# Attention with a gated dense layer on one core: another exponential polynomial on VectorE, sums in smaller parts, and 37 groups in place of 35

## The chip, the core and the metric

The kernel runs on one core of a Trainium2 chip. A core has five instruction streams: TensorE (PE, matrix products), VectorE (DVE), ScalarE (ACT), GpSimd (POOL) and SyncE (SP, which starts DMAs). Each runs its instructions in order, and they meet only at semaphores. The metric is the device time of one execution in microseconds (us). The kernel before takes 459.85 us, the median of 3 runs (459.81 to 459.92).

## The reference

For a sequence of S = 2048 rows of width D = 448, with H = 16 heads of 28 columns and a hidden width F = 1792:

```python
xn = layernorm(x)
q, k, v = split(xn @ wqkv)                       # 16 heads of 28
p = softmax(q @ k.T * 28 ** -0.5)                # per head, 2048 x 2048
s = (p @ v) @ wo
h = gelu(xn @ w1 + b1)                           # 2048 x 1792
g = silu(h @ w2 + b2)
out = x + s * g
```

## The kernel before, in words

**Tiles.** The 16 heads are four groups of four (g), the 2048 queries four chunks of 512 (c). One pair (g, c) is a block, 16 in all, block b = 4 g + c. In a block there are 16 key tiles t of 128 keys by 4 heads j, so 64 score tiles of 128 keys by 512 queries, numbered m; over all blocks 1024. The last block is cut into pieces of 256 and 128 queries, so that its sums end sooner. Four successive tiles, the four heads of one key tile, are a quad: quad q holds tiles 4q to 4q+3.

**Two ways to the exponential.** Scores are made on TensorE, four heads beside each other as row tiles, into PSUM (L1237, `t_score`). ScalarE takes the tiles of most quads in units of two or three (`p_exps`, L1293): one ACTIVATE with Exp from the PSUM ring to a bf16 slot in SBUF (P, or space of h and xnT that is free at the time). The quads listed in `QUADS` go to VectorE instead and are called late groups: 35 of 256. `p_late` gets a free PSUM bank for each of their tiles, `p_apass` (L1396) turns a tile into a bf16 bit pattern, by adding in the exponent's place, so that it reads as 2^i (1 + f), where i is the whole and f the fractional part of the scaled score. Four such tiles lie side by side in one buffer T of 128x2048. Then `p_expq` makes two more buffers of that size:

```python
W  = T & 0x407F                    # L1447: 2 (1 + f)
D1 = W * A3/4 + A2/2               # L1449
W  = W * D1                        # L1451: a polynomial in f
D1 = T & 0x7F80                    # L1452: 2^i
W  = W * T                         # L1454
```

The exponential is T + D1 + W. The three are not added on VectorE: TensorE sums all three with the same values v.

**Sums.** `p_pv` walks the tiles in steps of 8 (two quads), behind the exponentials. `pv_task` (matmuls at L1508) makes one task of TensorE from the 8 tiles and from the late groups of that block that are ready: 4 matmuls for a quad that ScalarE made, 12 for a late group. Heads lie side by side as column tiles of the accumulator `acc`, the weights are 32 columns of `vaug` (v of a head, and a column of 2.0 that gives the softmax's denominator). At a block's end `p_epi` copies `acc` out (L1566), takes the reciprocal (L1576), splits it on GpSimd into a high and a low bf16 part (rhi L1578, rlo L1579), and TensorE spreads it (L1588).

**Other work.** Projections of q, k, v (L748, L1039), the first dense layer (`p_f1`, L1101), the gelu in one stretch in the middle (`p_gelu`, L1150; it begins at the unit that reaches tile `GM` = 582), the second dense layer (`p_f2`, L1171; its result gets b2 added on VectorE, L1177), the output projection (L1605). All of these share two PSUM banks with the late groups' tiles; six banks are the ring with units of three and two tiles, one is `acc`. `p_busy` fills spare time of TensorE with matmuls that add zero to `acc` (L909), where the planner's count of its recent use is low.

**Order.** The program is written out when the kernel is built. `_Kernel.run` is a planner: it holds a set of processes, each of which offers its next task with an estimated duration, estimates the earliest start from when its operands are ready and its engine is free, and puts down the earliest (within `EPS` = 0.1 the one with the lowest priority number). The order on each engine is then fixed, and `deps` adds the semaphore waits. A changed duration or an added task thus moves the order of work on every engine. DMAs are issued at the point of the program where their process reaches them, most on SP.

**Buffers.** Late groups need three of the twelve units of `self.unit` (space of x, plx, w2, wq, wk and, once a head group is done, kT). They are free again when the group's sum is put down.

Of the kernel before, what the change touches and what calls it, by code (L numbers as in the profile page):

```python
# [8 lines left out]
ALU = mybir.AluOpType  # L9
# [10 lines left out]
C = 4  # L20
# [7 lines left out]
MTOT = NBLK * T * 4  # L28

GM = 64 * 9 + 6  # L30
QUADS = (17, 18, 25, 37, 41, 58, 68, 70, 81, 90, 97, 98, 117, 124, 131, 135, 140, 142, 146, 154, 157, 159, 161, 162, 165, 183, 185, 197, 200, 210, 211, 225, 229, 234, 242)
SM_SCALE = DH ** -0.5
LOG2E = 1.4426950408889634
EXP_A3, EXP_A2, EXP_LC = 0.16391228, 0.00783292, 1.1187538523466403
EXP_OFF = 64.0 / (LOG2E * SM_SCALE)
LN_EPS = 1e-5
KNORM = 2.5
# [11 lines left out]
JOINT = 0.05  # L49
LEAD, WAIT, GLEAD = 0, 3.0, 48  # L50
EPS = 0.1


class _Buf:
# [22 lines left out]
class _Kernel:  # L77
# [21 lines left out]
    def sb(self, name, shape, dtype=dt.bfloat16):  # L99
        return self.es.enter_context(self.nc.sbuf_tensor(name, shape, dtype))  # L100
# [163 lines left out]
    def alloc(self):  # L264
# [30 lines left out]
        self.colK = sb("colK", [128, G], f32)  # L295
        self.plx = sb("plx", [128, 2048], bf)
        self.coff = sb("coff", [128, 1], f32)
        self.b2b = sb("b2b", [128, D], bf)
        self.st6 = sb("st6", [128, T, 6], f32)
        self.mv = sb("mv", [128, T, 2], f32)  # L300
        self.lnv = sb("lnv", [128, T], f32)
# [49 lines left out]
        self.b_qT = [[B() for _ in range(C)] for _ in range(G)]  # L351
        self.b_onT = self.b_qT
        self.q_ready = [[False] * C for _ in range(G)]
        self.b_v = [[B() for _ in range(T)] for _ in range(2)]
        self.b_h = [B() for _ in range(C)]
        self.b_g = [B() for _ in range(C)]
# [33 lines left out]
    def schedule(self):  # L390
        K = self
        K.n_f1 = 0
        K.exp_u = -1
        K.exp_m = -1
        K.late_ready = []
        K.sc_u = -1
        K.pv_m = -1
        K.E_done = -1
        K.norms_done = False
        K.stg_done = 0  # L400
        K.pe_wait = 0
# [12 lines left out]
        K.next_m = 0  # L414
        K.n_late = 0
        K.gu = None
        K.pend = None
        K.units = []
        K.pv_done = [False] * MTOT
        K.late = {4 * q + k for q in QUADS for k in range(4)}  # L420
        K.late_left = [sum(1 for q in QUADS if K.sub_of(4 * q) == b) for b in range(NBLK + 3)]
        K.late_on = False
        K.PB, K.PPREV, K.plast = {}, {}, {}
        K.free_u = []
        K.a_left = {}
        K.ln2e = 0
        K.late_blk = 0
        K.banks += [(K.ring[:, b, :], K.b_ring[b]) for b in (3, 2)]
        K.outs = []
        K.gelu_done = False  # L430
        K.dir_n = 0
        K.dir_read = 0
        self.constants()
        self.loads()
        for c in range(C):
            K.spawn(K.p_ln(c), c)
        K.spawn(K.p_first(), 0)
# [24 lines left out]
        for c in range(C):  # L462
            K.spawn(K.p_k(1, c), nxt())
        K.spawn(K.p_q(1, 0), nxt())
        for t in range(T):
            K.spawn(K.p_v1(t), nxt())
        for c in (1, 2, 3):
            K.spawn(K.p_q(1, c), nxt())
        K.spawn(K.p_qn(1), nxt())
        f1 = deque(SBT)  # L470
        for c in range(C):
            for _ in range(4):
                K.spawn(K.p_f1(*f1.popleft()), nxt())
            K.spawn(K.p_k(2, c), nxt())
            K.spawn(K.p_q(2, c), nxt())
        K.spawn(K.p_qn(2), nxt())
        while f1:
            K.spawn(K.p_f1(*f1.popleft()), nxt())
        for c in range(C):
            K.spawn(K.p_k(3, c), nxt())  # L480
            K.spawn(K.p_q(3, c), nxt())
        K.spawn(K.p_qn(3), nxt())
        K.spawn(K.p_gelu(), 0)
        K.spawn(K.p_direct(), 0)
        for c in range(C):
# [104 lines left out]
    def loads(self):  # L590
# [20 lines left out]
            ld(K.x_sb[:, c, :, :], xr[c], K.s_x[c], [K.b_x[c]], 8.0 + 1.8 * c)  # L611
        lw(4 * DH, D, K.s_wqk1, K.b_stg1, 16.5)

        ld(K.b2b[:, :], K.B_b2.partition_broadcast(128), K.s_w["b"], [K.b_b2], 20)
        ld(K.w1[:, 0:3, :], K.B_w1[0:384, :].rearrange("(kt p) f -> p kt f", p=128), K.s_w["w1"], [], 0)
        ld(K.w1[0:64, 3, :], K.B_w1[384:448, :], K.s_w["w1"], [K.b_w1], 30)

# [7 lines left out]
        def late_w2():  # L625
# [4 lines left out]
                    K.b_w2.r += b.r + [b.w]  # L630
            ld(K.w2[:, :, :], K.B_w2.rearrange("(ft p) d -> p ft d", p=128), K.s_w["w2"], [K.b_w2], K.now + 14)
        K.spawn(late_w2(), 50)

        def pool_pads():
            yield ("until", lambda: K.stg_done == 2)
# [525 lines left out]
    def p_f2(self, c, t):  # L1161
# [5 lines left out]
        for q in range(7):  # L1167
            def f(eng, q=q):
                ins = None
                for ft in (2 * q, 2 * q + 1):  # L1170
# [3 lines left out]
            yield _Task(PE, f, [K.b_w2, K.b_h[c]], [tok], 0.378, 0.17)  # L1174
        K.pe_wait -= 1
        fb = K.fsb[:, c % 2, t, :]
        yield _Task(DVE, lambda eng: eng.tensor_tensor(fb, ps, K.b2b[:, :], ALU.add), [tok, K.b_b2], [K.b_fsb[c % 2]],  # L1177
                    0.63, 0.0, 2)
        K.banks.append((bank, tok))
        K.f2n[c] += 1  # L1180
# [251 lines left out]
    def p_expq(self, m0, u):  # L1432
        K = self
        b = K.sub_of(m0)
        uv = []
        yield ("until", lambda: K.ln2e == 0 and K.a_left[m0] == 0 and K.unit_of(b) is not None)
        K.ln2e = 1
        for _ in range(2):
            yield ("until", lambda: K.unit_of(b) is not None)
            v = K.unit_of(b)  # L1440
            K.free_u.remove(v)
            uv.append(v)
# [6 lines left out]
        yield _Task(DVE, lambda eng: eng.tensor_scalar(D1.bitcast(f16), W, EXP_A3 / 4.0, EXP_A2 / 2.0, op0=ALU.mult, op1=ALU.add),  # L1449
                    bW, bD, 0.69, 0.0, 4)  # L1450
        yield _Task(DVE, lambda eng: eng.tensor_tensor(W.bitcast(f16), W, D1.bitcast(f16), ALU.mult), bW + bD, bW, 1.22, 0.0, 4)  # L1451
        yield _Task(DVE, lambda eng: eng.tensor_scalar(D1.bitcast(u16), T.bitcast(u16), 0x7F80, None, op0=ALU.bitwise_and),  # L1452
                    bT + bW, bD, 0.69, 0.0, 4)
        yield _Task(DVE, lambda eng: eng.tensor_tensor(W, W.bitcast(f16), T, ALU.mult), bT + bW, bW, 1.22, 0.0, 4)  # L1454
        K.ln2e = 0
        K.late_ready.append((m0, (u, uv[0], uv[1])))

    def p_pv(self):
        K = self
# [27 lines left out]
    def pv_task(self, q, late, ms):  # L1487
# [2 lines left out]
        for x in late:  # L1490
            K.late_ready.remove(x)
        K.late_left[b] -= len(late)
        src = [(m,) + K.p_slot(m) for m in ms if m not in K.late]
        for m0, us in late:
            for u in us:
                src += [(m0 + k, K.unit[u][:, 512 * k:512 * k + 512], K.b_U[u][k]) for k in range(4)]
        n = len(src) / 4
        fl, rd = [], []
        for kk in range(4):
            for m, ap, tok in src:  # L1500
# [6 lines left out]
                def f(eng, t=t, j=j, g=g, q0=q0, nq=nq, col=col, ap=ap):  # L1507
                    return eng.matmul(K.acc[32 * j:32 * j + 32, q0:q0 + nq], K.vaug[:, t, 4 * g + j, :],  # L1508
                                      ap[:, col:col + nq], tile_position=(0, 32 * j), start=(t == 0),
                                      stop=(t == T - 1), skip_group_check=True)  # L1510
                fl.append(f)
                rd += [tok, K.b_v[0 if g == 0 else 1][t]]

        if not src:
            return
# [6 lines left out]
        yield _Task(PE, fall, rd, [K.b_acc], 0.223 * n + 0.001 * len(fl), 0.17,  # L1522
                    lambda: 1.2 if K.exp_m - K.pv_m > 20 or K.exp_m > MTOT - 12 or (K.gu is not None and K.gu - 1 <= K.exp_u <= K.gu) else 6, mode="col")
        for _, us in late:
            K.free_u += us

    def p_slot(self, m):
        i = self.PB[m]
# [170 lines left out]
```

## Time and profile before

| | |
|---|---|
| median of 3 runs | 459.85 us |
| profiled execution | 459.7 us |
| its span, first to last instruction | 457.9 us |
| ScalarE busy | 445.3 us, 97% |
| TensorE busy | 432.7 us, 94%, of which L909 35.1 |
| VectorE busy | 381.3 us, 83% |
| GpSimd busy | 45.0 us, 10% |
| first exponential starts, last ends | 12.59, 451.27 us |
| gelu with its two table loads | 247.96 to 275.85 us |
| TensorE's granted clock | 0.997 |

Times in the profile are counted from the first instruction. Busy time is the union of an engine's instructions; durations of neighbours on one engine overlap a little, so distances from start to start say more on throughput than mean durations. TensorE's ends are modelled. In rows of groups the fields are line, engine, operation, result and operands by name, their shapes, the count, then busy us and mean ns of one, then idle time of the engine just before them and what ended it. In a list of waits the fields after the colon are total us, count and the longest.

### The profile page before, as it was taken

The page shows a single profiled execution, that of the slowest core. Times are in us where ns is not written, and L with a number is a line of the kernel's source. Part 1 is how long each engine was busy: PE and PEld are TensorE (multiplying, and loading weights), DVE is VectorE, ACT ScalarE, POOL GpSimd, SP SyncE. Part 2 cuts the span into 40 slices and gives each one's busy share as a digit, 9 for nine tenths or more (in the row PEclk, how much of TensorE's full clock was granted, in tenths as well). Part 3 has the DMA queues.
Part 4 walks back from the last instruction along what each step waited for, and adds up shares of the span by engine and source line. Part 5 has one row for each costly group of instructions (what it writes and reads, how often), then busy time and mean ns, then how long its engine had stood idle before and what let it go on. Part 6 is the DMA issues. An engine that isn't in the chain of part 4 may idle for free.

```text
span 457.9 us, 10674 instructions
## 1 busy us (share of the span) xinstructions
PE 432.7 (94%) x4446; PEld 164.0 (36%) x4475; DVE 381.3 (83%) x593; ACT 445.3 (97%) x406; POOL 45.0 (10%) x85
## 2 busy tenths in 40 slices
PE   6999999999999999999999999999999999999995
PEld 4533334332223233223234333333233333343562
DVE  8956988886878888968899898889878798889865
ACT  6999999999999999999999999999999999999994
POOL 7470000000000100100000001010000100111012
PEclk9999999999999999999999999999999999999998
DMA  8701000000000000000040000000000000402012
GB/s 265 273 2 35 4 0 1 1 1 4 1 0 1 1 3 2 3 1 1 0 140 5 2 0 1 2 1 1 0 1 2 1 1 1 82 1 34 10 23 62
DMA packets 8049, 11.16 MB, mean 24 GB/s; under 512 B 1697, under 2 KB 6993, under 8 KB 7954
## 3 DMA queue, kind: packets, MB, share of 16 engines
q1 hardware_dynamic: 6850, 8.43, 5.8%
q0 software_dynamic: 864, 1.38, 2.4%
q8 instruction: 35, 0.57, 0.5%
q10 hardware_dynamic: 288, 0.69, 0.4%
q14 instruction: 12, 0.10, 0.1%
HBM read 8.61 MB, written 3.21 MB: 26 GB/s over the span
## 4 chain that ended last, share of the span: by engine, by line
PE 53%; ACT 31%; issue 11%; DVE 3%; DMA 1%; POOL 0%; ACTq 0%; DVEq 0%; POOLq 0%
PE ring L1237 16%; ACT P L1293 14%; PE acc L1508 9%; ACT h L1293 7%; ACT xnT L1293 7%; PE ring L1101 6%; PE ring L1171 4%; PE acc L909 4%; PE ring L748 3%; PE misc L1101 2%; PE misc L748 2%; PE misc L1039 1%; ACT h L1150 1%; PE misc L1171 1%; PE ring L1039 1%
## 5 line engine op out<-in xcount | busy, mean ns | idle before, releaser
L1293 ACT ACTIVATE P<-ring 128x1024 bf16<-128x1024 f32 (+1 forms) x186 | 214.8, 1267 | 1.4 <-PE ring L1237 1.3
L1237 PE MATMUL ring<-qT,kT 32*128 32x512 bf16 (+2 forms) x1075 | 145.4, 358 | 11.3 <-ACT P L1293 4.1
L1293 ACT ACTIVATE h<-ring 128x1024 bf16<-128x1024 f32 (+1 forms) x103 | 118.4, 1242 | 0.4 <-PE ring L1237 0.2
L1237 PEld LDWEIGHTS ring<-qT,kT 32*128 32x128 bf16 x1075 | 37.5, 91 | 133.0 <-ACT P L1293 52.6
L1293 ACT ACTIVATE xnT<-ring 128x1536 bf16<-128x1536 f32 (+1 forms) x71 | 82.4, 1282 | 0.1
L1508 PE MATMUL acc<-P,vaug 128*32 128x512 bf16 (+2 forms) x526 | 48.4, 356 | 0.0
L1101 PE MATMUL ring<-xnT,w 128*128 128x512 bf16 x152 | 40.6, 382 | 1.8 <-issue 1.1
L1578 POOL CAST rhi<-rc 128x16 bf16<-128x16 f32 x15 | 5.9, 394 | 357.6 <-DVE rc L1576 333.6
L1171 PE MATMUL ring<-w,h 128*128 128x448 bf16 x154 | 37.4, 355 | 0.0
L909 PE MATMUL acc<-ident,zero 128*128 128x128 bf16 x429 | 35.1, 220 | 0.0
L909 PEld LDWEIGHTS acc<-ident,zero 128*128 128x128 bf16 x429 | 24.3, 98 | 15.4 <-issue 14.5
L1237 PE MATMUL misc<-qT,kT 32*128 32x512 bf16 (+1 forms) x77 | 28.7, 377 | 0.0
L1508 PE MATMUL acc<-h,vaug 128*32 128x512 bf16 x250 | 28.0, 384 | 0.0
L1396 DVE TENSOR_SCALAR x_sb<-ring 128x512 uint16<-128x512 f32 x26 | 17.9, 687 | 2.8 <-PE ring L1237 2.6
L1101 PEld LDWEIGHTS ring<-xnT,w 128*128 128x128 bf16 x164 | 12.3, 97 | 20.1 <-issue 7.7
L1508 PE MATMUL acc<-xnT,vaug 128*32 128x512 bf16 (+2 forms) x232 | 18.1, 333 | 0.0
L1508 PEld LDWEIGHTS acc<-P,vaug 128*32 128x32 bf16 x526 | 12.0, 94 | 16.0 <-issue 13.4
L1566 DVE CAST E_sb<-acc 128x512 bf16<-128x512 f32 x15 | 10.4, 692 | 8.3 <-PE acc L1508 8.3
L1171 PEld LDWEIGHTS ring<-w,h 128*128 128x128 bf16 x154 | 11.2, 97 | 17.1 <-issue 10.3
L1396 DVE TENSOR_SCALAR kT<-misc 128x512 uint16<-128x512 f32 x20 | 13.8, 688 | 4.1 <-PE misc L1237 4.1
L1396 DVE TENSOR_SCALAR x_sb<-misc 128x512 uint16<-128x512 f32 x22 | 15.1, 686 | 2.4 <-PE misc L1237 2.1
L1101 PE MATMUL misc<-xnT,w 128*128 128x512 bf16 x54 | 15.9, 382 | 0.9 <-issue 0.6
(281 smaller groups left out, 682.1 us busy)
## 6 DMA issues: line engine op xcount, KB each, us to landing
w<-in_B_w_dram SPq DMA_DIRECT2D x1, 1568.0 KB, 7.4
w<-in_B_w_dram SPq DMA_DIRECT2D x1, 1344.0 KB, 8.2
out_dram<-in_A_x_dram SPq DMA_DIRECT2D x3, 448.0 KB, 11.2
out_dram<-h POOLq DMA_DIRECT2D x6, 224.0 KB, 3.9
x_sb<-in_A_x_dram SPq DMA_DIRECT2D x2, 448.0 KB, 5.8
h<-in_A_wqkv_dram SPq DMA_DIRECT2D x3, 168.0 KB, 4.9
x_sb<-in_A_x_dram ACTq DMA_DIRECT2D x1, 448.0 KB, 4.4
h<-in_A_x_dram SPq DMA_DIRECT2D x1, 448.0 KB, 3.4
```

Source lines behind the costliest of these rows:

```text
L748: ins = eng.matmul(bank, w[:, kt, g * 128:(g + 1) * 128], K.xnT[:, kt, c * 512:(c + 1) * 512], start=(kt == 0), stop=(kt == KT - 1))
L909: ins = eng.matmul(K.acc[:, 0:128], K.zero[:, :], K.ident[:, :], start=False, stop=True, skip_group_check=True)
L1039: ins = eng.matmul(bank[:, off:off + nh * 32], K.xnT[:, kt, t * 128:(t + 1) * 128], ap, start=(kt == 0), stop=(kt == KT - 1), skip_group_c ...
L1101: ins = eng.matmul(bank, K.w1[:, kt, ft * 128:(ft + 1) * 128], K.xnT[:, kt, c * 512:(c + 1) * 512], start=(kt == 0), stop=(kt == KT - 1))
L1150: yield _Task(ACT, lambda eng, dst=dst, src=src: eng.activation(dst, src, ACTF.Gelu_apprx_tanh), rd, wr, 0.4267 * n + (0.1 if pc else 0.06 ...
L1171: ins = eng.matmul(ps, hv[:, ft, t * 128:(t + 1) * 128], K.w2[:, ft, :], start=(ft == 0), stop=(ft == FT - 1))
L1237: return eng.matmul(dst, K.kT[32 * j:32 * j + 32, g, t * 128:(t + 1) * 128], K.qT[32 * j:32 * j + 32, g, c * 512 + q0:c * 512 + q0 + nq], ...
L1293: return eng.activation(reg[:, i0:i0 + n, :], K.ring[:, b0:b0 + n, :], ACTF.Exp, scale=SM_SCALE)
L1396: yield _Task(DVE, lambda eng: eng.tensor_scalar(K.unit[u][:, 512 * k:512 * k + 512].bitcast(dt.uint16), bank, SM_SCALE * LOG2E * 128.0, ( ...
L1508: return eng.matmul(K.acc[32 * j:32 * j + 32, q0:q0 + nq], K.vaug[:, t, 4 * g + j, :], ap[:, col:col + nq], tile_position=(0, 32 * j), sta ...
L1566: yield _Task(DVE, lambda eng: eng.tensor_copy(E, K.acc[:, :]), [K.b_acc], [tE], 0.7, 0.0, 0)
L1578: yield _Task(POOL, lambda eng: eng.tensor_copy(K.rhi[:, :], K.rc[:, :]), [K.b_rc], [K.b_rhl], 1.1, 0.0, 1)
```

## The change

The polynomial becomes 2^i (1 + m + c m^3) with m = 1 + f (not the tile number) and c = 0.167. `p_expq` then needs two masks and two products, and no multiply-add: D1 = W W, W = D1 T, D1 = T & 0x7F80. The factor c/4 of the third operand isn't applied to W but to the values: `p_cv`, a new process on GpSimd, writes c/4 times the four heads' values of the group's key tile into one of four slots `cv` (two slots for a group of the last block), and the sum of W uses those as its weights. A late group begins its polynomial only once such slots are free and its values are there; the slots come free with the units.

The sum task is cut: `pv_task` still collects the same tiles, but gives them to `t_pv` in parts of at most `4 * PVN` = 8 tiles (two operand groups of four), each a task of its own, between which the planner may put others.

`QUADS` is a new list of 37 groups. `b2b` (b2 spread over the partitions) loses its own buffer and lies in that of `wv`; its load moves from the start to after the last use of `wv`.

```diff
-QUADS = (17, 18, 25, 37, 41, 58, 68, 70, 81, 90, 97, 98, 117, 124, 131, 135, 140, 142, 146, 154, 157, 159, 161, 162, 165, 183, 185, 197, 200, 210, 211, 225, 229, 234, 242)
+QUADS = (17, 21, 24, 33, 39, 49, 52, 66, 75, 85, 86, 98, 100, 114, 124, 134, 138, 142, 146, 153, 154, 155, 161, 162, 171, 178, 179, 189, 194, 197, 206, 210, 211, 225, 227, 237, 243)
-EXP_A3, EXP_A2, EXP_LC = 0.16391228, 0.00783292, 1.1187538523466403
+EXP_C, EXP_LC = 0.1669921875, 1.1155446
+NCV = 4
+PVN = 2
...
-        self.b2b = sb("b2b", [128, D], bf)
+        self.b2b = self.wv[:, 0, 0:D]
+        self.cv = sb("cv", [128, NCV, 128], bf)
...
-        ld(K.b2b[:, :], K.B_b2.partition_broadcast(128), K.s_w["b"], [K.b_b2], 20)
...
+        def late_b2():
+            yield ("until", lambda: all(x.tw is not None for x in K.b_v[1]))
+            K.b_b2.r += K.b_wv.r + K.b_wvpad.r + [K.b_wv.w, K.b_wvpad.w]
+            ld(K.b2b, K.B_b2.partition_broadcast(128), K.s_w["b"], [K.b_b2], K.now + 6)
+        K.spawn(late_b2(), 50)
...
-        yield ("until", lambda: K.ln2e == 0 and K.a_left[m0] == 0 and K.unit_of(b) is not None)
+        room = lambda: [i for i in range(0, NCV, len(pc)) if all(k in K.free_cv for k in range(i, i + len(pc)))]
+        yield ("until", lambda: K.ln2e == 0 and K.a_left[m0] == 0 and K.unit_of(b) is not None and room()
+               and all(bv[p[0]].tw is not None for p in pc))
...
+        K.spawn(K.p_cv(cs, [p[0] for p in pc], g, bv), m0)
...
-        yield _Task(DVE, lambda eng: eng.tensor_scalar(D1.bitcast(f16), W, EXP_A3 / 4.0, EXP_A2 / 2.0, op0=ALU.mult, op1=ALU.add),
-                    bW, bD, 0.69, 0.0, 4)
-        yield _Task(DVE, lambda eng: eng.tensor_tensor(W.bitcast(f16), W, D1.bitcast(f16), ALU.mult), bW + bD, bW, 1.22, 0.0, 4)
+        yield _Task(DVE, lambda eng: eng.tensor_tensor(D1.bitcast(f16), W, W, ALU.mult), bW, bD, 1.22, 0.0, 4)
+        yield _Task(DVE, lambda eng: eng.tensor_tensor(W, D1.bitcast(f16), T, ALU.mult), bT + bD, bW, 1.22, 0.0, 4)
...
-        yield _Task(DVE, lambda eng: eng.tensor_tensor(W, W.bitcast(f16), T, ALU.mult), bT + bW, bW, 1.22, 0.0, 4)
...
+    def p_cv(self, cs, ts, g, bv):
+        K = self
+        for i, t in zip(cs, ts):
+            yield _Task(POOL, lambda eng, i=i, t=t: eng.tensor_scalar(
+                K.cv[:, i, :], K.vaug[:, t, 4 * g:4 * g + 4, :].rearrange("p h e -> p (h e)"), EXP_C / 4.0, None, op0=ALU.mult),
+                [bv[t]], [K.b_cv[i]], 0.8)
...
+        for i in range(0, len(src), 4 * PVN):
+            yield self.t_pv(q, src[i:i + 4 * PVN])
+        for _, us, cs in late:
+            K.free_u += us
+            K.free_cv += cs
...
+                w = K.vaug[:, t, 4 * g + j, :] if cs is None else K.cv[:, cs[kk], 32 * j:32 * j + 32]
```

More of the change, by code (lines that the diff above doesn't have):

```diff
@@ L353, in alloc @@
         self.q_ready = [[False] * C for _ in range(G)]
+        self.b_cv = [B() for _ in range(NCV)]
         self.b_v = [[B() for _ in range(T)] for _ in range(2)]
@@ L424, in schedule @@
         K.free_u = []
+        K.free_cv = list(range(NCV))
         K.a_left = {}
@@ L1176, in p_f2 @@
         fb = K.fsb[:, c % 2, t, :]
-        yield _Task(DVE, lambda eng: eng.tensor_tensor(fb, ps, K.b2b[:, :], ALU.add), [tok, K.b_b2], [K.b_fsb[c % 2]],
+        yield _Task(DVE, lambda eng: eng.tensor_tensor(fb, ps, K.b2b, ALU.add), [tok, K.b_b2], [K.b_fsb[c % 2]],
                     0.63, 0.0, 2)
@@ L1435, in p_expq @@
         uv = []
-        yield ("until", lambda: K.ln2e == 0 and K.a_left[m0] == 0 and K.unit_of(b) is not None)
-        K.ln2e = 1
+        _, _, pc, _, _ = K.pieces(m0)
+        bv = K.b_v[0 if m0 // 64 < C else 1]
+        room = lambda: [i for i in range(0, NCV, len(pc)) if all(k in K.free_cv for k in range(i, i + len(pc)))]
+        yield ("until", lambda: K.ln2e == 0 and K.a_left[m0] == 0 and K.unit_of(b) is not None and room()
+               and all(bv[p[0]].tw is not None for p in pc))
+        K.ln2e = 1
+        cs = list(range(room()[0], room()[0] + len(pc)))
+        for i in cs:
+            K.free_cv.remove(i)
+        g = m0 // 64 // C
+        K.spawn(K.p_cv(cs, [p[0] for p in pc], g, bv), m0)
         for _ in range(2):
@@ L1448, in p_expq @@
                     bT, bW, 0.69, 0.0, 4)
-        yield _Task(DVE, lambda eng: eng.tensor_scalar(D1.bitcast(f16), W, EXP_A3 / 4.0, EXP_A2 / 2.0, op0=ALU.mult, op1=ALU.add),
-                    bW, bD, 0.69, 0.0, 4)
-        yield _Task(DVE, lambda eng: eng.tensor_tensor(W.bitcast(f16), W, D1.bitcast(f16), ALU.mult), bW + bD, bW, 1.22, 0.0, 4)
+        yield _Task(DVE, lambda eng: eng.tensor_tensor(D1.bitcast(f16), W, W, ALU.mult), bW, bD, 1.22, 0.0, 4)
+        yield _Task(DVE, lambda eng: eng.tensor_tensor(W, D1.bitcast(f16), T, ALU.mult), bT + bD, bW, 1.22, 0.0, 4)
         yield _Task(DVE, lambda eng: eng.tensor_scalar(D1.bitcast(u16), T.bitcast(u16), 0x7F80, None, op0=ALU.bitwise_and),
                     bT + bW, bD, 0.69, 0.0, 4)
-        yield _Task(DVE, lambda eng: eng.tensor_tensor(W, W.bitcast(f16), T, ALU.mult), bT + bW, bW, 1.22, 0.0, 4)
         K.ln2e = 0
-        K.late_ready.append((m0, (u, uv[0], uv[1])))
+        K.late_ready.append((m0, (u, uv[0], uv[1]), cs))
+    def p_cv(self, cs, ts, g, bv):
[4 more added lines that the diff above has]
+                [bv[t]], [K.b_cv[i]], 0.8)
     def p_pv(self):
@@ L1492, in pv_task, with t_pv @@
         K.late_left[b] -= len(late)
-        src = [(m,) + K.p_slot(m) for m in ms if m not in K.late]
-        for m0, us in late:
+        src = [(m,) + K.p_slot(m) + (None,) for m in ms if m not in K.late]
+        for m0, us, cs in late:
             for u in us:
-                src += [(m0 + k, K.unit[u][:, 512 * k:512 * k + 512], K.b_U[u][k]) for k in range(4)]
+                src += [(m0 + k, K.unit[u][:, 512 * k:512 * k + 512], K.b_U[u][k], cs if u == us[2] else None) for k in range(4)]
+        for i in range(0, len(src), 4 * PVN):
[3 more added lines that the diff above has]
+            K.free_cv += cs
+    def t_pv(self, q, src):
+        K = self
         n = len(src) / 4
@@ L1499, in pv_task @@
         for kk in range(4):
-            for m, ap, tok in src:
+            for m, ap, tok, cs in src:
                 _, j, pc, _, s = K.pieces(m)
@@ L1505, in pv_task, with f @@
                 t, q0, nq, col = pc[kk]
-                def f(eng, t=t, j=j, g=g, q0=q0, nq=nq, col=col, ap=ap):
-                    return eng.matmul(K.acc[32 * j:32 * j + 32, q0:q0 + nq], K.vaug[:, t, 4 * g + j, :],
+                w = K.vaug[:, t, 4 * g + j, :] if cs is None else K.cv[:, cs[kk], 32 * j:32 * j + 32]
+                def f(eng, t=t, j=j, w=w, q0=q0, nq=nq, col=col, ap=ap):
+                    return eng.matmul(K.acc[32 * j:32 * j + 32, q0:q0 + nq], w,
                                       ap[:, col:col + nq], tile_position=(0, 32 * j), start=(t == 0),
@@ L1511, in pv_task @@
                 fl.append(f)
-                rd += [tok, K.b_v[0 if g == 0 else 1][t]]
-        if not src:
-            return
+                rd += [tok, K.b_v[0 if g == 0 else 1][t] if cs is None else K.b_cv[cs[kk]]]
         def fall(eng, fl=fl):
@@ L1521, in fall @@
             return ins
-        yield _Task(PE, fall, rd, [K.b_acc], 0.223 * n + 0.001 * len(fl), 0.17,
+        return _Task(PE, fall, rd, [K.b_acc], 0.223 * n + 0.001 * len(fl), 0.17,
                     lambda: 1.2 if K.exp_m - K.pv_m > 20 or K.exp_m > MTOT - 12 or (K.gu is not None and K.gu - 1 <= K.exp_u <= K.gu) else 6, mode="col")
-        for _, us in late:
-            K.free_u += us
     def p_slot(self, m):
```

## The prediction

> **What bounds the kernel now.** I read the page's busy shares first, then the table of stretches, ScalarE's waits, the groups by shape, and the timelines around ScalarE's gaps. The table of stretches gives, for each stretch in us, its length and the busy time of TensorE (PE), its weight loads (PEld), VectorE (DVE), ScalarE (ACT) and GpSimd (POOL):
>
> ```profile
> 0.00:15.00 15.00, 10.43 (x92) 7.61 (x93) 12.62 (x46) 10.06 (x25) 10.62 (x31) 1.00 0.85 269
> ...
> 180.00:245.00 65.00, 61.42 (x615) 20.63 (x622) 54.76 (x83) 65.00 (x58) 2.57 (x6) 1.00 0.09 26
> 245.00:276.00 31.00, 30.33 (x192) 10.99 (x191) 28.80 (x40) 30.94 (x23) 0.00 (x0) 1.00 0.00 1
> 276.00:340.00 64.00, 62.87 (x596) 21.55 (x592) 54.30 (x73) 63.97 (x56) 2.91 (x6) 1.00 0.01 1
> ...
> 445.00:458.00 13.00, 7.70 (x167) 4.29 (x163) 7.47 (x16) 6.74 (x7) 3.05 (x3) 0.89 0.28 59
> ```
>
> ScalarE is full from 15 to 445 us (idle sum of those stretches about 1.5 us). VectorE has some 10 us of idle in each 64 us and GpSimd is nearly empty. So the end is set by the first exponential (12.59 us), ScalarE's stream of work, and the chain after the last exponential at 451.27 us (6.6 us: sum, reciprocal, projection, store). ScalarE's own waits say the same; the one wait inside the stream, for scores, is 1.5 us in all:
>
> ```profile
> ACT P L678 <- DMA x_sb<-in_A_x_dram: 2.2, 1, 2.2
> ACT P L1293 <- PE ring L1237: 1.3, 4, 0.5
> ...
> ACT h L1293 <- PE ring L1237: 0.2, 1, 0.2
> ```
>
> The exponentials by shape (count, then busy us and mean ns), of two and three score tiles of 128x512 each:
>
> ```profile
> L1293 ACT ACTIVATE P<-ring 128x1536 bf16<-128x1536 f32 x85 | 127.4, 1499 | 0.4 <-PE ring L1237 0.3
> L1293 ACT ACTIVATE P<-ring 128x1024 bf16<-128x1024 f32 x101 | 105.5, 1071 | 1.1 <-PE ring L1237 1.0
> ```
>
> With the rows that write h and xnT there are 85+44+35 = 164 of three and 101+59+36 = 196 of two: 884 of the 1024 tiles, the other 140 being VectorE's 35 groups. Neighbours overlap, so the price is start to start: an undisturbed exponential of two takes 0.904 us and of three 1.330 us (medians over the start times in ScalarE's timeline). 196 and 164 of these make 395.3 us; the pitches recorded sum to about 8 us more. About 1.3 us of that is small work between them at the start, the rest hiccups too short to show as idle.
>
> **What the skill says.** "SBUF — State Buffer", section "SBUF: two separate sides": VectorE and GpSimd share a port pair as an exclusive lock, held for a whole instruction, and the loser blocks. The trace agrees: GpSimd's small step rlo takes 0.22 us alone, and 1.21 us where it meets the 1.23 us product.
>
> ```profile
> 183.34 1.23 DVE L1451 TENSOR_TENSOR x_sb<-x_sb,w 128x2048 f16<-128x2048 bf16 x1
> ...
> 183.43 1.21 POOL L1579 TENSOR_TENSOR rlo<-rc,rhi 128x16 bf16<-128x16 f32 x1
> ```
>
> "TensorEngine Tiling (Array Packing)", "Key Properties": a change of tiling mode drains TensorE. In the trace a sum starts 0.31 us after a score's start, 0.1 us more than 512 columns need (0.213 us apart in a row of sums). "VectorE: DVE Perf Modes", "Side-by-side: where the cycles go for N=2048 bf16": 1224 ns for a two-input operation, 693 ns for a one-input one; the rows below agree.
>
> **The change, part by part.**
>
> *Two more groups.* 8 score tiles leave ScalarE: two exponentials of three and one of two, 2 x 1.330 + 0.904 = 3.56 us. All other ScalarE work stays. In both lists 18 groups lie before the gelu (tile 582), so all of this saving falls after 275.85 us, where 17 groups become 19.
>
> *VectorE's polynomial.*
>
> ```profile
> L1396 DVE TENSOR_SCALAR x_sb<-ring 128x512 uint16<-128x512 f32 x26 | 17.9, 687 | 2.8 <-PE ring L1237 2.6
> L1449 DVE TENSOR_SCALAR x_sb<-kT 128x2048 f16<-128x2048 bf16 x6 | 4.1, 681 | 0.1
> L1451 DVE TENSOR_TENSOR kT<-kT,x_sb 128x2048 f16<-128x2048 bf16 x6 | 7.3, 1217 | 0.0
> ```
>
> A group costs 4 x 0.687 for its score tiles, three one-input passes of 0.69 and two products of 1.22: 7.26 us. The pass of L1449 goes, the products stay two, 16-bit in and out as before: 6.57 us. In all 35 x 7.26 = 254.1 becomes 37 x 6.57 = 243.1, 11 us less. It is worth nothing by itself, since VectorE isn't the bound; it makes room for the two groups. After the gelu the balance is 17 x 7.26 = 123.4 against 19 x 6.57 = 124.8: 1.4 us more, beside about 27 us of idle there.
>
> *Scaled values on GpSimd.* 37 groups, 38 passes of 128x128 (one group lies in the last block and has two). The trace lacks this shape: a 128x128 copy (selb) took 0.29 us, a 128x128 comparison (ident) 0.62. I take 0.35; with the lock a pass may be held by each VectorE operation that it meets. Low end 0.3 us, hidden; high end the whole sequence, 3.8 us. Even then it is ready no later than the group's last operand (D1), since both start together; the sum waits for that anyway. Ahead of rhi and rlo in GpSimd's queue it can delay an epilogue, and TensorE behind its broadcast L1588, by up to about 1.5 us: a chance in some one or two of 15 blocks. The other side of the lock: 38 x 0.35 = 13 us of VectorE held at worst, against 77 us of idle; so hidden too. No recorded VectorE duration is longer beside GpSimd work.
>
> *TensorE.* Each group adds 8 sum tiles beyond those that its P tiles would need: 2 x 8 x 0.213 / 4 columns side by side = 0.85 us, and its scores, part of them taken along with ScalarE's, up to 2 x 4 x 0.22 = 1.8 us less 0.7 for three exponentials' scores. Cover: the filling matmuls (L909), 429 of 0.055 us = 24 us, of which about 12 us after the gelu.
>
> *Sums in parts.* In TensorE's order of work there are 45 unbroken runs of sums over 8 matmuls (16 of 12, 10 of 16, 18 of 20, one of 40), so about 64 new cuts. Where nothing slips in, a cut is free; where a score does, it costs two drains, 0.2 us: 0 to 13 us of TensorE, under that cover. The gain: a run of 20 takes 1.07 us and can hold a score back. At 78.5 us it does, and ScalarE loses 0.38 us:
>
> ```profile
> 78.52 0.62 PE L1508 MATMUL acc<-P,vaug 128*32 128x512 bf16 x8
> ...
> 79.72 0.62 PE L1237 MATMUL ring<-qT,kT 32*128 32x512 bf16 x6
> ...
> 80.17 1.45 ACT L1293 ACTIVATE P<-ring 128x1536 bf16<-128x1536 f32 x1 [0.27 <-PE ring L1237]
> ```
>
> Of ScalarE's hiccups over 0.07 us, ten come with a run of 12 or more, 2.2 us together, one of 0.37 at the gelu's table load perhaps not for that reason. So the parts are worth between 0 and -2 us; the new order of everything can bring hiccups of about 1 us. I take -0.6 net.
>
> *b2's load.* It goes from SP's early queue (0.61 us of issue at 8.45) to behind the last use of wv near 96 us. SP then waits there; behind it is only the next write to qT, issued at 108.7. W1's load, next in the early queue, starts 0.6 us sooner. VectorE reads b2 after 276 us. Nothing on the path: 0, either way below 0.2.
>
> *Sum*: profiled execution 459.7 (span 457.9) - 3.56 - 0.6 = 455.5; the median of the runs shown is 0.15 above the profiled time, so 455.6 us.
>
> **Rivals.** (1) *Half the gain is eaten*: two groups more after the gelu, where TensorE shows 62.87 of 64.00 us busy, give late scores. Loss of 1.5 to 3 us of new hiccups: 457 to 458.9. For it: the dense TensorE; against it: filling matmuls still fit there (27 up to 340 us), and projections can slide to 400-445, where 144 of them stand. (2) *No change* (458.9 to 460.8): TensorE's drains use up the cover, and what ScalarE loses equals the 3.56 us; I see no stretch dense enough for that. (3) *Slower*: GpSimd's passes arrive late, because the lock lets them in only after the polynomial and they then take over 1 us, and TensorE stands at a sum for them with the scores queued behind it. Only two units of scores are buffered, so a stop hurts ScalarE from about 0.5 us on. 37 stops lose over 3.56 us once each holds ScalarE by over 0.1 us, a stop of 0.6 us. With 1 us each: 37 x 0.5 - 3.6 = 15 us slower, 470. Against it: GpSimd got in between VectorE operations in every case seen, so the pass should end some 2 us ahead of its sum. (4) *More gain*: nearly all hiccups of long runs vanish too, 453.7.
>
> **How the numbers follow.** Forecast with its own range 454.2 to 457: 0.62. Rival 1: 0.18. No change: 0.05. Slower: 0.09. More gain: 0.06. Under 0.2% (0.9 us) two medians of this kernel can't be told apart; so faster 0.86, same 0.05, slower 0.09. The range 453.8 to 458.6 holds the forecast, most of rival 1 and nearly all of rival 4, leaving out about 0.18.
>
> **What would show it.** Right: ScalarE's exponentials are 162 of three and about 195 of two, its time from the first exponential after the gelu to the last falls from 175.4 to about 172 us, the gelu begins within 1 us of 247.96, VectorE's busy time falls to about 370, L1508's runs are at most 8 long between scores, and the tail after the last exponential stays 6.6 us. Wrong: idle of ScalarE or of sums waiting for the scaled values by more than 1 us in all; passes on GpSimd over 3 us; VectorE's products off 1.22 us; or hiccups after the gelu growing by more than 2 us.

## The result, and the profile after

The changed kernel takes 458.55 us (median of 4 runs, 458.24 to 459.04) against 459.88 us of the kernel before on the same chip: ratio 0.997, interval 0.9953 to 0.9988. It is faster, by 1.3 us, where 4.3 us had been forecast. Run once more on another occasion it took 458.28 us against 459.97, ratio 0.9964 (0.9952 to 0.9977).

The profiled executions are 459.7 us before (span 457.9) and 458.85 us after (span 457.0), so the spans differ by 0.9 us. ScalarE is the engine that is full from the first exponential to the last, so its own landmarks cut the span into five pieces: up to the first exponential, on to the table load of the gelu, the gelu up to the first exponential behind it, on to the end of the last exponential, and the tail.

| us | first exp | before the gelu | gelu | after the gelu | tail | span |
|---|---|---|---|---|---|---|
| before | 12.59 | 235.36 | 27.89 | 175.43 | 6.63 | 457.90 |
| after | 12.87 | 234.60 | 30.19 | 171.78 | 7.54 | 456.97 |
| difference | +0.28 | -0.76 | +2.30 | -3.65 | +0.91 | -0.93 |

The expected saving is there (-3.65), and two thirds of it are given back in the gelu stretch. The first column is not the change's: over the runs below it lies between 12.56 and 13.16, and the two executions of the changed kernel have 12.87 and 12.75.

The stretches of the changed kernel, columns as before:

```profile
245.00:276.00 31.00, 30.03 (x213) 11.11 (x215) 28.03 (x38) 28.97 (x21) 4.59 (x7) 1.00 0.00 1
276.00:340.00 64.00, 63.12 (x541) 20.95 (x539) 46.78 (x63) 63.84 (x57) 6.79 (x10) 1.00 0.01 1
```

From 245 to 276 us ScalarE was busy for 30.94 us before and is for 28.97 now. Its waits name the place; the first line is new:

```profile
ACT h L1160 <- PE ring L1111: 2.0, 2, 1.1
ACT P L1303 <- PE ring L1247: 1.0, 3, 0.5
```

L1160 is the gelu, L1111 the first dense layer. The gelu reads 34 of its 56 tiles from h in SBUF, where they were put earlier, and 22 "direct" ones straight from the ring; in that stretch TensorE must make those 22 while ScalarE works through the rest. The end of the gelu, ScalarE's timeline (start, length, instruction, idle before it and what ended it), before:

```profile
270.75 1.52 ACT L1150 ACTIVATE h<-h 128x1536 bf16<-128x1536 bf16 x1
272.13 2.40 ACT L1150 ACTIVATE h<-ring 128x1536 bf16<-128x1536 f32 x2
```

and after:

```profile
270.39 1.48 ACT L1160 ACTIVATE h<-h 128x1536 bf16<-128x1536 bf16 x1
272.74 1.45 ACT L1160 ACTIVATE h<-ring 128x1536 bf16<-128x1536 f32 x1 [0.88 <-PE ring L1111]
275.32 1.02 ACT L1160 ACTIVATE h<-ring 128x1024 bf16<-128x1024 f32 x1 [1.12 <-PE ring L1111]
```

The last two direct units come late. Before, TensorE made their 20 matmuls in one run (second line: L1101 from 268.87 to 273.36), with 16 sum matmuls behind them:

```profile
268.56 0.39 PE L1237 MATMUL misc<-qT,kT 32*128 32x512 bf16 x1
268.87 4.49 PE L1101 MATMUL ring<-xnT,w 128*128 128x512 bf16 x20
273.30 0.40 PE L1508 MATMUL acc<-P,vaug 128*32 128x512 bf16 x4
```

After, the same matmuls are parted by the epilogue of block 8 (L1617, eight pieces, of which one is shown) and by 12 sum matmuls:

```profile
268.76 2.33 PE L1111 MATMUL ring<-xnT,w 128*128 128x512 bf16 x10
271.03 0.24 PE L1617 MATMUL ring<-ident,rhi 128*32 128x128 bf16 x4
...
271.81 1.67 PE L1111 MATMUL ring<-xnT,w 128*128 128x512 bf16 x7 [0.16 <-issue]
273.42 0.40 PE L1542 MATMUL acc<-wk,vaug 128*32 128x512 bf16 x4
273.65 0.39 PE L1542 MATMUL acc<-x_sb,vaug 128*32 128x512 bf16 x4
273.86 0.39 PE L1542 MATMUL acc<-plx,cv 128*32 128x512 bf16 x4
274.18 1.04 PE L1111 MATMUL ring<-xnT,w 128*128 128x512 bf16 x4
```

In TensorE's order, between the first and the last direct matmul, there stood 36 sum matmuls and no epilogue before; now 60 and 36 epilogue matmuls. An estimate from the trace: the 24 more sum matmuls take 24 x 0.053 = 1.3 us (four columns share 0.213), the epilogue 0.5, and five more changes of tiling mode (30 against 25 between those two matmuls) at the prediction's 0.1 us another 0.5. Together these are the 2.3 us. Block 8, with three late groups (quads 134, 138, 142) in place of four (131, 135, 140, 142), now ends inside the gelu; before, it ended behind it (the step rhi of that block ran at 282.38, now at 268.43). That the list is the reason isn't shown: in e2 below, with the four groups of before, rhi ran at 272.85, inside the gelu too.

### The profile page after: what moved, and what is told of

Same layout as the page of the kernel before. It is cut to its first block, busy times and chain, and to the rows that moved or that the text cites. A ratio compares the mean times of both kernels' runs of the same rounds, so it can differ in the third digit from the quotient of the medians.

```text
span 457.0 us, 10602 instructions
## 1 busy us (share of the span) xinstructions
PE 432.2 (95%) x4397; PEld 160.6 (35%) x4428; DVE 369.8 (81%) x574; ACT 441.1 (97%) x403; POOL 70.0 (15%) x123
## 4 chain that ended last, share of the span: by engine, by line
PE 62%; ACT 24%; issue 9%; DVE 4%; POOL 1%; ACTq 0%; DVEq 0%; POOLq 0%
PE ring L1247 18%; ACT P L1303 14%; PE acc L1542 12%; ACT h L1303 8%; PE misc L1181 7%; PE ring L1111 6%; PE acc L919 4%; PE ring L1181 3%; PE ring L758 2%; PE misc L1111 1%; PE misc L758 1%; ACT xnT L1303 1%; PE misc L1634 1%; PE ring L1634 1%; PE acc L901 1%
## 5 line engine op out<-in xcount | busy, mean ns | idle before, releaser
L1303 ACT ACTIVATE xnT<-ring 128x1536 bf16<-128x1536 f32 (+1 forms) x68 | 78.9, 1294 | 0.4 <-PE ring L1247 0.4
L1111 PE MATMUL ring<-xnT,w 128*128 128x512 bf16 x164 | 44.5, 381 | 2.7 <-issue 1.4
L1478 POOL TENSOR_SCALAR cv<-vaug 128x128 bf16<-128x128 bf16 x38 | 24.6, 646 | 138.3 <-PE acc L1542 136.4
L1181 PE MATMUL misc<-w,h 128*128 128x448 bf16 x154 | 37.6, 356 | 0.0
L919 PE MATMUL acc<-ident,zero 128*128 128x128 bf16 x366 | 31.0, 220 | 0.0
L919 PEld LDWEIGHTS acc<-ident,zero 128*128 128x128 bf16 x366 | 21.1, 98 | 14.6 <-issue 12.9
L1406 DVE TENSOR_SCALAR kT<-ring 128x512 uint16<-128x512 f32 x27 | 18.6, 689 | 4.6 <-PE ring L1247 4.5
L1111 PEld LDWEIGHTS ring<-xnT,w 128*128 128x128 bf16 x180 | 13.4, 97 | 21.9 <-issue 8.2
L1406 DVE TENSOR_SCALAR w<-misc 128x512 uint16<-128x512 f32 x18 | 12.4, 689 | 8.4 <-PE misc L1247 8.3
L1094 DVE CAST h<-ring 128x512 bf16<-128x512 f32 x23 | 15.8, 686 | 2.8 <-PE ring L1111 2.6
L1181 PEld LDWEIGHTS misc<-w,h 128*128 128x128 bf16 x154 | 11.2, 97 | 18.4 <-issue 11.1
```

What stands on the lines that cost most here:

```text
L919: ins = eng.matmul(K.acc[:, 0:128], K.zero[:, :], K.ident[:, :], start=False, stop=True, skip_group_check=True)
L1094: yield _Task(DVE, lambda eng: eng.tensor_copy(dst, bank), [tok], wr, 0.69, 0.0, 2)
L1111: ins = eng.matmul(bank, K.w1[:, kt, ft * 128:(ft + 1) * 128], K.xnT[:, kt, c * 512:(c + 1) * 512], start=(kt == 0), stop=(kt == KT - 1))
L1181: ins = eng.matmul(ps, hv[:, ft, t * 128:(t + 1) * 128], K.w2[:, ft, :], start=(ft == 0), stop=(ft == FT - 1))
L1303: return eng.activation(reg[:, i0:i0 + n, :], K.ring[:, b0:b0 + n, :], ACTF.Exp, scale=SM_SCALE)
L1406: yield _Task(DVE, lambda eng: eng.tensor_scalar(K.unit[u][:, 512 * k:512 * k + 512].bitcast(dt.uint16), bank, SM_SCALE * LOG2E * 128.0, ( ...
```

## The experiments

Theory A: the gelu stretch is set by TensorE, and the sums and the epilogue that now stand between the direct tiles lengthen it. Rivals: the cuts and the drains at the changes of tiling mode that they bring do (B), the list alone does (C), the scaled values on GpSimd hold TensorE (D), or the direct tiles are late for a reason outside TensorE (E).

**Each part undone alone.** First the sums uncut, with list and polynomial kept:

```diff
-PVN = 2
+PVN = 64
```

> The changed kernel with its sums uncut (up to 64 operand groups in a task); 37 groups and the new polynomial stay. Theory A (the gelu stretch is set by TensorE: the sums and block 8's epilogue that stand between the direct dense tiles lengthen it): its order has the same 60 sum matmuls and 36 epilogue matmuls there, so the stretch stays at 30.2 us (29.7 to 30.7). Rival B (the cuts and their drains lengthen it): back to 28.5 us or less. The stretch before the gelu should lose what the cuts gave, 234.6 to 235 or more. Total 458.5 to 459.5 by A, 457 by B.

Measured: 468.76 us, ratio to the kernel before 1.0191 (1.0176 to 1.0206). The gelu took 30.67 us, as A says, with the same 60 sum and 36 epilogue matmuls and 29 changes of tiling mode between its direct tiles, so the cuts aren't what makes it long (against B). But before it there are 238.85 us and after it 177.84.

The list of before in the changed kernel:

> The changed kernel with the 35 groups of before; polynomial and cuts stay. Theory A: 48 sum matmuls and 36 epilogue matmuls between the direct tiles, gelu stretch 29.4 to 29.9 us; after the gelu 175.4 us as before; total about 461.5, slower than before. Rival C (the new list alone is what lengthens the gelu): stretch 27.9, total 459.3.

Measured: 462.50 us, ratio 1.0056 (1.0040 to 1.0073). Gelu 31.30 us, after it 175.04. So the gelu is long without the new list (against C); A's direction held, its size was 1.4 us too small. TensorE also stood for 0.99 us before 262.19, waiting for the gelu to read a ring bank; that may be a part of it.

The cuts alone, in the kernel before:

```diff
+        for i in range(0, len(src), 4 * PVN):
+            yield self.t_pv(q, src[i:i + 4 * PVN])
```

> The kernel before with its sums cut in parts of two operand groups, nothing else. Theory A: 52 sum matmuls but only 4 epilogue matmuls between the direct tiles, gelu stretch 28.5 to 29.2 us. Rival B (cuts and drains): 29.8 or more. Before the gelu 0.5 to 1 us shorter than 235.4, after it 174.5 to 175.4. Total 459.3 to 460.3.

Measured: 465.93 us, ratio 1.0128 (1.0113 to 1.0143). Gelu 30.25 us, not 28.5 to 29.2: this one speaks for B as much as for A. Before the gelu nothing was gained (235.31). Its changes of tiling mode between the direct tiles are 31 against 25: here the cuts do bring some, by the same 0.1 us an estimate of 0.6 us. The tail is 9.95 us: behind the last exponential VectorE has five additions of output projections to make (L1617) where before it had one (L1614).

The list alone, in the kernel before:

> The kernel before with the new list of 37 groups, old polynomial, no scaled values, uncut sums. Theory A: 48 sum matmuls, 36 epilogue matmuls and 8 of the second layer between the direct tiles, gelu stretch 29.7 to 30.3 us. Rival D (the scaled values on GpSimd are what TensorE waits for): back to 28. After the gelu 171.9 us if VectorE has room for 19 groups at 7.26 us each, more by up to 2 us if not. Total 457.8 to 460.

Measured: 473.15 us, ratio 1.0289 (1.0273 to 1.0304). Gelu 30.23 us with no scaled values at all, against D. The list alone is thus enough to lengthen it, as the cuts alone were in e3, though neither is needed. After the gelu 183.05 us, 9 us beyond what I had allowed. ScalarE's waits for sums in the whole run, of which three of the four, 10.2 us, lie behind the gelu:

```profile
ACT P L1293 <- PE acc L1508: 8.6, 3, 4.2
ACT xnT L1293 <- PE acc L1508: 4.1, 1, 4.1
```

These are not waits for scores (that would be the ring, L1237) but for sums: an exponential can't be written until the sum that read its slot's last tile is done. One of the four, in the timeline of all engines but the weight loads:

```profile
395.42 2.69 PE L909 MATMUL acc<-ident,zero 128*128 128x128 bf16 x45
...
395.62 0.68 DVE L1452 TENSOR_SCALAR x_sb<-x_sb 128x2048 uint16<-128x2048 uint16 x1
...
396.34 1.23 DVE L1454 TENSOR_TENSOR kT<-kT,x_sb 128x2048 bf16<-128x2048 f16 x1
...
398.27 0.60 PE L1508 MATMUL acc<-x_sb,vaug 128*32 128x512 bf16 x8
...
398.70 0.39 PE L1508 MATMUL acc<-kT,vaug 128*32 128x512 bf16 x4
...
399.22 1.45 ACT L1293 ACTIVATE P<-ring 128x1536 bf16<-128x1536 f32 x1 [4.18 <-PE acc L1508]
399.40 0.69 DVE L1566 CAST E_sb<-acc 128x512 bf16<-128x512 f32 x1 [0.50 <-PE acc L909]
```

The block's sum (it ends in the copy L1566) waits for the last polynomial product of a late group (L1454, into kT), TensorE fills the time with L909, and ScalarE stands for 4.18 us. The filling matmuls stand ahead of that sum in TensorE's order; the sum begins 0.5 us behind the product's end, so they hold it by no more than that. VectorE had been busy for 12.50 of the 13.57 us from 384 to the product's end. So VectorE, whose shorter polynomial the prediction had as "worth nothing by itself", bounds the end of this block, where its groups follow one another closely. e1, with the new polynomial, has one stop of 3.9 us for a sum too; what held that sum was not taken apart.

These four point to one thing that none of the theories had said: a list of groups fits only the order for which it was chosen. Each of the four is 4 to 15 us slower than the changed kernel. What the parts are worth one by one can't be read from such runs; the next two keep the order.

**Taking the work away in place.** The planner's durations stay, so that every instruction stands where it stood, but the sums of the gelu stretch and block 8's epilogue are made short; their results are not complete.

```diff
                 t, q0, nq, col = pc[kk]
+                nq = nq if not K.in_gelu() else 64
...
-                        ins = eng.matmul(bank2[32 * j:32 * j + 32, 128 * q:128 * (q + 1)],
-                                         r[:, 4 * q + j:4 * q + j + 1].to_broadcast([128, 32]), K.ident[:, :],
+                        n = 16 if b == 8 else 128
+                        ins = eng.matmul(bank2[32 * j:32 * j + 32, 128 * q:128 * q + n],
+                                         r[:, 4 * q + j:4 * q + j + 1].to_broadcast([128, 32]), K.ident[:, 0:n],
```

> The changed kernel, every instruction in the same order, but the sums put down during the gelu stretch run over 64 columns instead of 512 and the spreading matmuls of block 8's epilogue over 16 instead of 128; it leaves the rest of those sums out. Theory A (TensorE is short of time in the gelu stretch, because of these sums and this epilogue): some 3 us of TensorE go, the waits of ScalarE for direct dense tiles (2.0 us) vanish, the stretch falls from 30.2 to 27.9 to 28.4 us, total 456.2 to 456.8. Rival E (the direct tiles are late for another reason: ring banks that come free late, VectorE, or the scaled values): stretch stays at 29.7 or more, total within 0.5 of 458.5.

Measured: 456.43 us, ratio to the kernel before 0.9922 (0.9907 to 0.9936). The pieces: 234.60, 28.21, 171.77, tail 7.52. Behind the first exponential only the gelu stretch changed by more than 0.02 us, namely by 1.98, and of ScalarE's wait for direct tiles this is left:

```profile
ACT h L1160 <- PE ring L1111: 0.2, 1, 0.2
```

That settles A against E: TensorE is short of time there, and the time that sums and epilogue take is enough to account for it. It does not bound the drains: the order and its 30 changes of tiling mode were the same, but the time that the shorter sums give back covers them too. What speaks against the cuts as their cause is e1.

**The tail.** GpSimd's two operations of the last silu, a product and an addition, shortened to 16 of 448 columns, in the same order; the rest of that tile is left out.

> The changed kernel in the same order, but GpSimd's two products of the last silu, after the last exponential, run over 16 columns instead of 448; the rest of that tile is left out. Theory F (the lock: GpSimd's product holds VectorE's two-input addition L1647 for 0.6 us, and the copy of the last sum stands behind it): L1647 at the end takes 0.39 us instead of 1.00, the tail after the last exponential falls from 7.5 to 6.9 us, total 0.2 to 0.6 us below 458.5, and its runs spread less than 458.2 to 459.0. Rival: the tail stays at 7.5 because TensorE's clock at the end is what differs.

Measured: 458.43 us (457.94 to 458.53), ratio to the kernel before 0.9963 (0.9948 to 0.9977). The tail fell from 7.54 to 6.97 us, as F says; the total does not show it, since it lies within the spread of the changed kernel's own, and this profile's first exponential came at 13.12. In the timeline of the changed kernel GpSimd starts first and VectorE's addition beside it is long (the second L1647 line):

```profile
449.28 0.39 DVE L1647 TENSOR_TENSOR h<-h 128x448 bf16<-128x448 bf16 x1
449.59 0.62 DVE L1643 TENSOR_TENSOR h<-misc,h 128x448 bf16<-128x448 f32 x1
...
449.97 1.03 POOL L1215 TENSOR_TENSOR h<-w 128x448 bf16<-128x448 bf16 x1 [5.18 <-ACT w L1213]
...
450.25 1.00 DVE L1647 TENSOR_TENSOR h<-h 128x448 bf16<-128x448 bf16 x1
...
451.17 0.28 DVE L1569 CAST E_sb<-acc 128x128 bf16<-128x128 f32 x1
```

The addition ends just behind GpSimd's product, 0.6 us late, and the copy of the last sum stands behind it. The same timeline with the short product:

```profile
450.22 0.21 POOL L1215 TENSOR_TENSOR h<-w 128x16 bf16<-128x16 bf16 x1 [5.18 <-ACT w L1213]
...
450.49 0.39 DVE L1647 TENSOR_TENSOR h<-h 128x448 bf16<-128x448 bf16 x1
...
451.04 0.29 DVE L1569 CAST E_sb<-acc 128x128 bf16<-128x128 f32 x1 [0.15 <-PE acc L919]
```

Before, VectorE's addition was the first of the two and took 0.39 us:

```profile
451.70 0.39 DVE L1618 TENSOR_TENSOR h<-h 128x448 bf16<-128x448 bf16 x1
451.82 1.16 POOL L1205 TENSOR_TENSOR h<-w 128x448 bf16<-128x448 bf16 x1 [2.00 <-ACT w L1203]
```

The 0.9 us by which the changed kernel's tail is longer have three parts. Its repeat has a tail of 7.34 us with the addition at 1.00 us too, and a last projection of 0.36 us, as in x2 and before; against that, the short product saves 0.37 us. That is less than the 0.6 us of the addition, since the copy then waits for TensorE (the 0.15 above). Another 0.2 us is the last projection of the first profile, one matmul of 0.55 us instead of 0.36; the granted clock of that stretch was 0.80 instead of 0.89, but that this is why isn't shown. The last 0.34 us (6.97 against 6.63) lie in front of the copy: the last sums start 0.41 us behind the end of the last exponential, before 0.05. Why they do stays open.

**The direct tiles first.** One priority in the planner:

```diff
-                    yield K.t_f1((f0 + n) // FT, (f0 + n) % FT, K.ring[:, b0 + n, :], K.b_ring[b0 + n], k, 3.5)
+                    yield K.t_f1((f0 + n) // FT, (f0 + n) % FT, K.ring[:, b0 + n, :], K.b_ring[b0 + n], k, 0.5)
```

> The changed kernel with the direct dense tiles of the gelu stretch ahead of the sums in the planner's priorities (0.5 instead of 3.5). Theory A: gelu stretch 27.9 to 28.6 us. What the sums then owe is paid after the gelu, and the list was not chosen for this order: the stretch after the gelu lengthens from 171.8 to between 173 and 177; total 458 to 463. If the list hardly matters, after the gelu stays 171.8 and the total is 456.3.

Measured: 464.56 us, ratio 1.0088 (1.0071 to 1.0106). The gelu takes 27.90 us, the direct tiles are in time; after it there are 178.89 us instead of 171.78, more than I had allowed. ScalarE's waits of this run are again for sums, and for VectorE's addition of b2:

```profile
ACT P L1303 <- PE acc L1542: 3.7, 2, 2.4
ACT w L1197 <- DVE w L1187: 2.8, 2, 1.5
```

**Lists chosen anew.** If the list is what fails, a list for the new order should bring the gain through. Three runs: two lists of 37 with the direct tiles first (v1, v2), and one of 39 for uncut sums (u1). Each was found by trying many lists in the planner with that order's settings and keeping one with an early end. In the first two the last silu's product is one VectorE operation behind the last reciprocal's product, instead of two on GpSimd.

```diff
+            yield ("until", lambda: K.on4[3])
-            yield _Task(POOL, lambda eng: eng.tensor_tensor(o, sg[:, 3, :], fb[:, 3, :], ALU.mult),
-                        [K.b_sig3, K.b_fsb[c % 2]], [K.b_h[c], K.b_g3], 0.85, 0.05, 0)
-            yield _Task(POOL, lambda eng: eng.tensor_tensor(o, o, fb[:, 3, :], ALU.add),
-                        [K.b_fsb[c % 2]], [K.b_h[c], K.b_g3], 0.85, 0.05, 0)
+            yield _Task(DVE, lambda eng: eng.scalar_tensor_tensor(o, sg[:, 3, :], 1.0, fb[:, 3, :], op0=ALU.add, op1=ALU.mult),
+                        [K.b_sig3, K.b_fsb[c % 2]], [K.b_h[c], K.b_g3], 0.62, 0.0, 4)
...
+QUADS = (17, 21, 25, 34, 38, 49, 52, 66, 75, 81, 90, 98, 99, 113, 124, 131, 133, 137, 147, 150, 152, 154, 160, 161, 171, 176, 179, 188, 194, 196, 203, 209, 216, 226, 231, 235, 244)
```

The lists of v2 and of u1:

```python
QUADS = (17, 20, 22, 34, 38, 49, 52, 67, 69, 85, 96, 97, 100, 116, 124, 132, 137, 146, 149, 151, 153, 154, 160, 161, 170, 176, 177, 185, 192, 197, 208, 212, 216, 225, 230, 236, 244)
QUADS = (17, 21, 22, 32, 33, 49, 52, 66, 75, 83, 86, 89, 97, 103, 114, 128, 134, 137, 146, 147, 151, 154, 155, 157, 158, 162, 167, 176, 177, 188, 193, 199, 206, 208, 216, 227, 230, 232, 244)
```

> The changed kernel with the direct dense tiles ahead of the sums in the gelu stretch, the last silu's product on VectorE behind the last reciprocal's product instead of on GpSimd, and a list of 37 groups chosen anew for this order. Theory A, with the finding that a list fits only the order that it was chosen for: gelu stretch 27.9 us, before it 234.5, after it 171 to 173, tail 6.5 to 6.9; total 454.5 to 456.5, faster than both kernels. Rival (the chip's order of events departs from the planner's, and a stop of ScalarE comes anyway): 457 to 462.

> The same with another list of 37, chosen anew in the same way, with 18 or 19 groups before the gelu. By A: gelu stretch 27.9, total 454.5 to 456.5; by the rival a total apart from the other list's by over 3 us.

> The changed kernel with uncut sums, and a list of 39 groups chosen anew for that order. If the loss of e1 (468.8) came from a list that didn't fit: 458 to 461. If uncut sums as such cost it: 465 or more. Gelu stretch 30 to 32, since the sums stand ahead of the direct tiles here.

> The changed kernel once more, for a comparison on the same chip. Same medians within 0.5: 458.2 to 458.9; gelu stretch 30.2. Its tail is 7.5 us where GpSimd's last product holds VectorE's addition, and 6.9 where it doesn't: the profile shows which.

| | median us | ratio to the kernel before (interval) | before the gelu | gelu | after the gelu | tail |
|---|---|---|---|---|---|---|
| v1, direct first, own list | 455.66 | 0.9905 (0.9890 to 0.9920) | 234.38 | 27.89 | 171.87 | 6.99 |
| v2, the same, list b | 456.20 | 0.9920 (0.9907 to 0.9934) | 237.19 | 27.89 | 169.70 | 6.99 |
| u1, uncut, own list of 39 | 458.47 | 0.9967 (0.9955 to 0.9979) | 236.82 | 31.21 | 169.19 | 6.82 |
| the changed kernel again | 458.28 | 0.9964 (0.9952 to 0.9977) | 234.61 | 30.19 | 171.78 | 7.34 |

v1 beats both kernels: 4.3 us below the kernel before, 2.6 below the repeat of the changed one. Of the 2.6, the gelu is 2.3 and the tail, with the silu's product on VectorE, 0.35. ScalarE's timeline of it has no wait for direct tiles:

```profile
270.34 1.52 ACT L1160 ACTIVATE h<-h 128x1536 bf16<-128x1536 bf16 x1
271.71 2.40 ACT L1160 ACTIVATE h<-ring 128x1536 bf16<-128x1536 f32 x2
274.14 1.28 ACT L1164 ACT_TABLE_LOAD   x1
```

v2 has one group fewer before the gelu than v1 (17, where 18 or 19 had been expected) and one more behind it, so a pair of its pieces differs from v1's, by 2.8 us more and 2.2 less; their sums differ by 0.6. u1 shows that e1's loss of 10 us was for the most part the list's: with a list of its own the uncut kernel is as fast as the cut one, within the intervals. But that list has two groups more, which by the prediction's price take another 3.56 us from ScalarE. That the uncut order would be as fast with 37 groups is not shown.

## Why the prediction was wrong

The forecast was 455.6 us with a range of 453.8 to 458.6. The direction was right and 458.55 lies just inside the edge of the range; the size was over three times too large. By its own steps:

*Two more groups, -3.56 us: right.* After the gelu ScalarE spends 3.65 us less, on 72 exponentials of three and 74 of two instead of 74 and 75. The gelu's table load came at 247.47, within the 1 us stated.

*VectorE's polynomial, 11 us less: right in size.* Busy time fell from 381.3 to 369.8 us. "It is worth nothing by itself" was too short: e4 shows what the same list costs when the polynomial keeps its fifth pass, though in another order.

*Scaled values hidden: right.* 38 passes, median 0.53 us (0.35 had been taken), longest 1.66 us; the list of TensorE's waits has none for a value, and GpSimd itself waits only for a slot to come free. The lock did cost something, but elsewhere. "No recorded VectorE duration is longer beside GpSimd work" was not so even in the kernel before: of ten steps L710 with a median of 0.395 us, one took 0.71 us at 20.06 us, beside a GpSimd step (L714) that had started 0.22 us earlier. In the tail after, such a step lies on the path to the end. "SBUF — State Buffer", "SBUF: two separate sides", says that whichever starts first holds the pair; in the tail the order of the two flipped, and I had priced the lock only for the new passes.

*The tail stays 6.6 us: wrong*, by 0.9 us, of which the lock is 0.4.

*TensorE: the failed step.* Its added work was set against a cover of "about 12 us after the gelu" and 24 us in all. The cover is a sum over the kernel, the need is local: in the gelu stretch the table of stretches that I quoted shows TensorE busy for 30.33 of 31.00 us, with filling matmuls of 1.1 us, all of them ahead of the first direct tile, and there the direct tiles are due at fixed times. I quoted that row and put rival 1's loss into the stretch behind it. The sums and the epilogue that moved in between the direct tiles were paid by ScalarE: 2.3 us of the 3.0 us missing to the forecast; the rest is about what the tail lost. Nor did I ask which blocks' ends the new order moves: block 8's went from behind the gelu into it.

*Sums in parts, -0.6 net: not decided.* Before the gelu the changed kernel gained 0.76 us. But its runs of sums are not "at most 8 long": the last block's apart, 41 are longer, where 45 were, since parts stand one behind another; the runs of 20 fell from 18 to one. That 0.76 is near the forecast's figure may be luck. u1 reaches the same total uncut, with two groups more, and loses its time in other pieces, and e3 gained nothing before the gelu. An order-keeping test of the cuts isn't possible, since to be worth something a cut must let other work in; what they are worth stays open.

Rival 1 named the right engine and about the right size (457 to 458.9), at the wrong place and by another mechanism: not late scores behind the gelu, but late direct tiles in it. That the cuts (B) aren't needed for it is shown by e1; in e3, where the gelu was 1 us longer than A's figure, the changes of tiling mode that the cuts brought are an estimated 0.6 us, and the rest is open.

## What to carry to other kernels

Where one engine is full throughout, ask stretch by stretch which engine would be next, and whether the change moves work into the stretch where that engine has nothing to spare; cover added up over the whole kernel does not count there. A list or schedule that was chosen for one order is a part of that order: undoing one edit alone then measures mostly the misfit, and what an edit does is better seen by shortening its work in place or by choosing the list again. Where two engines share a port, ask not only what the new operations cost but also which of the two a new order lets start first.

## What the runs showed that had not been expected

A VectorE addition of 128x448 with two SBUF inputs, 0.39 us, took 1.00 us where GpSimd's product had started 0.28 us before it. Every profile that has the two beside each other agrees: 1.00 to 1.04 us where GpSimd started first (the changed kernel, its repeat, e3, e5, x1), 0.39 us where VectorE did (before, u1). And an exponential can wait 4 us for a sum (e4): a late group at a block's end holds first TensorE's sum, then the slots that the sum has still to read, then ScalarE.
